# Set 0's block merge and the first units' decay factors on VectorE, with a new set of ranks

## The chip, the cores and the metric

One core of a Trainium2 chip. The metric is the device time of one execution, in microseconds; the kernel before takes 836.14 us (median of 3 runs, 835.84 to 836.43).

## The reference, cut to what matters

A recurrence over 768 time steps for 4 batches of 8 heads (head size 40), and behind it a two-part MLP with residuals.

```
for t in range(S):                                    # r k v w a b: (4, 8, 768, 40)
    y[:, :, t] = einsum('bhd,bhde->bhe', r_t, state)
    Sa = einsum('bhde,bhe->bhd', state, a_t)
    state = state * w_t[:, :, None, :] - einsum('bhd,bhe->bhde', Sa, b_t) + einsum('bhd,bhe->bhde', v_t, k_t)
x = y.transpose(0, 2, 1, 3).reshape(4, 768, 320)
h = relu(x^T @ w_tok1) @ w_tok2                       # over the 768 time steps, 256 wide
u = x + h^T
out = u + relu(u @ w_ch1) @ w_ch2                     # over the 320 features, 1536 wide
```

## The kernel before, in words

The 768 steps of each batch are cut into 12 chunks of 64, so there are 48 chunks, numbered g. Inside a chunk the recurrence becomes matrix products; between chunks a state is handed on, so the chunks of a batch form a chain.

**Preparation (`t_prep`, line 473).** The chunks are prepared in three units of 16, each in four quarters of 16 steps. A quarter loads a tile `pin`, scans the decays to running products (line 542), forms the reciprocal decay factors RC in one first step (line 567) and seven steps, each the one after it times a decay (line 569), multiplies K and B with RC and A with the running products (all of them through `either`, line 415), and stores the results to DRAM. `p_rc`, `p_k` and `p_a` say for each unit which engine does the factors, the products of K and B, and that of A: 0 is VectorE, 1 is POOL, 2 is whichever of POOL and VectorE is free. Units 0 and 1 feed chunks 0 to 31.

**Sets (`t_solve`, line 929).** Chunks go in six sets of 8. For a set, the diagonal 32-blocks of a triangular matrix of each chunk and head, in the buffer `Dg`, are transposed on VectorE (line 945) and inverted there: 15 row steps, each a product and a sum (lines 968 and 970), give the two 16-blocks of each 32-block. Then the 16-blocks are merged to 32-blocks. For sets from `pem` on, VectorE does it: six left pairs (983, 985), one copy (1004) and six right pairs (996, 999), and then the transposes to TBt (1024) and TBn (1029); `Dg` is free for the next set as soon as it is transposed. For sets below `pem` (before: set 0 alone) the left and right pairs are left out, and `t_merge` (line 883) does the merge after the transposes with small matmuls (line 898), which VectorE evicts (904) and adds (921, 922); `Dg` is free for the next set only after the first of these matmuls. The steps of a set have ranks that rise evenly from the set's own rank over `solve_span`:

```
steps += [left(e, 4 * e, t, t + 8) for e in range(2) for t in (0, 8)] + [left(e, 4 * e, 0, 16) for e in (2, 3)]
steps += rows + [right(e, 4 * e, 4 * e + 4) for e in range(2)]
...
    yield rank0 + K["solve_span"] * u / len(steps)
```

**Chunks.** `t_ab` (751) loads a pair of chunks, transposes and multiplies (pk, pa, px); `t_a` (830) evicts to Dg, N and AT; `t_b` (1111) copies the set's inverse to TBD (line 1129 and on), forms the pe, pt and ph products and evicts them. `t_chain` (1224) is the chain over the chunks, in two halves of the heads; its first matmuls are line 1259. `t_y` forms the output of a pair of chunks. `t_v` (1092) copies v on an engine out of `vg`. `t_conv` (line 1465) splits the MLP's weights from 64-bit words on POOL, ScalarE, VectorE and TensorE (lines 1497 to 1516), and `t_mlp` runs the MLP of one batch, with most of its matmuls in lines 1642 and 1756.

**The order.** `Planner` (line 74) runs all of this as generators before anything is on the chip. Each operation has an engine, a length and the rank of its task. Step by step the engine that can start soonest takes the ready operation with the lowest rank (TensorE adds a price for a change of matmul form, `aff`, `affx`), and what it takes is issued: the order on every engine's queue is that of the plan. Lengths are the planner's own estimates. A length marked `Port` also keeps other operations so marked waiting until it ends, on VectorE or POOL. Where TensorE would stand in the plan, `fill` issues small matmuls to a spare bank (line 402). All ranks, spans and engine choices are in the dict `K`.

Of the kernel before, what the change touches and what calls it, by code (L numbers as in the profile page):

```python
# [23 lines left out]
LAT = {"PE": 190.0, "ACT": 210.0, "DVE": 130.0, "POOL": 150.0, "SP": 1000.0, "SWD": 1100.0}  # L24


K = dict(mgs=0, mgl=0, lat=[200.0, 150.0, 145.0, 90.0], aff=[2.14563, 1.17505], affx=[1.41848, 1.75913],
         aff_g=12.71949, sets=[8, 8, 8, 8, 8, 8], atn=6, kbp=2, ld=3.64466, ldk=-0.09022, v=5.95243, vg='PDA',
         tbd_early=55.14308, tbd=[['DP', 'AD', 'DP', 'PA'], ['AP', 'P', 'PD', 'AP']], alt_c=1, slack=-24704.48396,
         evm=31.10979, p_rc=[2, 2, 2], p_a=[0, 0, 2], p_k=[0, 0, 1], solve=[5.47355, 2.30103, 3.06635, -7.67957,  # L30
         3.37784, -15.13123], solve_span=13.30881, atomic=0, a=10.15159, a_span=3.80664, b=1.43321, chain=0.31813,
         evac=17.1625, y=-0.05033, utr=-7.4913, pem=1, mrg=-1.4447, ea=7.7058, prp=17, psp=8, w=3, c=2, m=2, warm=0,
         fill=2, prep=[-17.22917, -0.28798, 24.97603], prep_step=[1.61428, -1.4801, -0.20849], p_wg=[1, 3], p_big=[2],
         mlp=[11.95325, 26.40847, 34.1668, 39.83709], mlp_span=[14.39104, 11.00328, 13.05494, 18.79706],
         conv_t=5.14066, conv_t_span=3.01188, conv_c=5.76098, conv_c_span=7.60449, conv_after=4, cv_free=2, cvp=[1,
         2], ub=0, y_ld=5.29409, e_k=-39.43453, e_a=-28.4508, e_s=2.43935, e_x=-25.441, e_l=-7.61654)


class Port(float):
# [31 lines left out]
class Planner:  # L71
# [105 lines left out]
    def away(self, form, rank):  # L177
# [3 lines left out]
        late = rank >= K["aff_g"]  # L181
        return K["affx"][late] if "A" not in (form, self.form) else K["aff"][late]

# [78 lines left out]
def tile_kernel(ctx, tc, r, k, v, w, a, b, wt1, wt2, wc1, wc2, wakb, rvt, vtok, wl, out, dbg=None):  # L262
    nc = tc.nc
    B, H, S, D = r.shape
# [8 lines left out]
    DP = 104  # L273
# [11 lines left out]
    prep = rec.enter_context(tc.tile_pool(name="prep", bufs=2))  # L285
# [96 lines left out]
    P = Planner()  # L382
# [90 lines left out]
    def t_prep(u):  # L473
# [7 lines left out]
        now = yield pr0  # L481
        for q in range(NQ):
# [12 lines left out]
            if u == 1 and q == NQ - 1:  # L495
                now = yield None
# [7 lines left out]
            def comp(q=q, d=d, ring=ring, tsl=tsl):  # L504
# [5 lines left out]
                now = yield None  # L510
# [27 lines left out]
                def scan():  # L538
                    if not alt:
# [2 lines left out]
                    nc.vector.tensor_tensor_scan(  # L542
                        out=o["CP"].rearrange("p e t -> p (e t)"), data0=pin[:, 0:W1N],
                        data1=D1.rearrange("p e t -> p (e t)"), initial=0.0, op0=ALU.mult, op1=ALU.add)
                now = yield [("DVE", Port(250), carry), ("DVE", 1560, scan)]
                P.set(scan_ev[q], now)
                CP, ce, fl = d["CP"], o["ce"], o["fl"]

# [28 lines left out]
                now = yield [("ACT", 760, sq), ("DVE", Port(190), rec), ("DVE", 650, lambda: nc.vector.reciprocal(out=d["rq"], in_=d["rq"]))]  # L577
# [20 lines left out]
                now = yield None  # L598
                P.spawn(rest(), pr0 + q * prs, now)

                now = yield [("ACT", 1225, lambda: nc.scalar.copy(out=W, in_=Pv))]
                P.set(cp_free[q], now)
                yield ld_ev
                now = yield [either(eng_a, lambda: A, lambda: A, lambda: W, ALU.mult, 640)]
# [10 lines left out]
                now = yield None  # L615
# [7 lines left out]
            now = yield None  # L623
# [16 lines left out]
        now = yield [("ACT", 160, pcc), ("ACT", 160, pcc2)]  # L640
        P.rel(tk, now)
        P.rel(R_cp, now)
        for s_ in stored:
            yield s_
        now = yield None
        P.set(prep_done[u], now)
        yield 12.0 * u
        now = yield [("DVE", 402, lambda: nc.vector.tensor_reduce(out=fl[:, 4:5], in_=ce, axis=AX.XY, op=ALU.min)),
               ("DVE", 402, lambda: nc.vector.tensor_reduce(out=fl[:, 5:6], in_=ce, axis=AX.XY, op=ALU.max)),
               ("DVE", 73, lambda: nc.vector.tensor_reduce(out=fl[:, 6:7], in_=fl[:, 0:NQ], axis=AX.X, op=ALU.max)),  # L650
               ("DVE", 70, lambda: check(u, 0, fl[:, 4:5], ALU.is_ge, CMAX ** -2, HL)),
               ("DVE", 70, lambda: check(u, 1, fl[:, 5:6], ALU.is_le, CMAX ** 2, HL)),
               ("DVE", 70, lambda: check(u, 2, fl[:, 6:7], ALU.is_le, WMAX ** 2, HL))]
# [811 lines left out]
    def t_conv(i, key, shape, sW, data, r0, r1):  # L1465
# [8 lines left out]
        now = yield None  # L1474
# [6 lines left out]
        else:  # L1481
            n = DM if kind == "c2" else 384
# [3 lines left out]
        def piece(j, hc, lc, n):  # L1486
            yield r0 + (r1 - r0) * j / len(ps_)
            yield R_hid
            buf = mp.tile([128, 2 * 384], F32, tag="hid", name=f"cx_{key[0]}_{key[1]}_{j}", bufs=HIDN)
            x = buf.bitcast(I32)[:, 0:2 * n]  # L1490
            xv = x.rearrange("p (n two) -> p n two", two=2)
            c, l = t_[:, hc:hc + n], t_[:, lc:lc + n]
            hi = xv[:, :, 1].bitcast(F32)
            a0 = c_ + 128 * n * j
            yield [("SP", (480.0, 3.6 * n), lambda: nc.sync.dma_start(out=x, in_=wl[a0:a0 + 128 * n].bitcast(I32).rearrange("(p n) -> p n", p=128)))]
            hI = xv[:, :, 1]
            yield [[(e, ns, lambda e=e: engines[e].tensor_scalar(out=c, in0=hi, scalar1=0.0, scalar2=None, op0=ALU.mult))  # L1497
                    for e, ns in (("POOL", 900.0), ("DVE", Port(68 + n)))][:K["cvp"][0]]]
            yield [("ACT", 95 + 0.97 * n, lambda: nc.scalar.activation(out=hi, in_=hi, func=AF.Copy, scale=2.0 ** -112))]
            yield [("DVE", Port(dve(n)), lambda: nc.vector.scalar_tensor_tensor(out=hI, in0=hI, scalar=3, in1=c.bitcast(I32),  # L1500
                                                                          op0=ALU.logical_shift_left, op1=ALU.bitwise_or))]
            pt, tk = yield from bank("m", [128, 384], f"cv_{key[0]}_{key[1]}_{j}")
            yield [[("ACT", 95 + 0.97 * n, lambda: nc.scalar.copy(out=c, in_=hi)),
                    ("POOL", 700, lambda: nc.gpsimd.tensor_copy(out=c, in_=hi))][:K["cvp"][1]],
                   ("DVE", 68 + n, lambda: nc.vector.tensor_scalar(out=pt[:, 0:n].bitcast(I32), in0=hI, scalar1=-0x800000, scalar2=None,
                                                                   op0=ALU.bitwise_and))]
            yield [("DVE", 60 + n / 0.96, lambda: nc.vector.scalar_tensor_tensor(
                out=l, in0=xv[:, :, 0].bitcast(U32), scalar=-2.0 ** -52, in1=pt[:, 0:n], op0=ALU.mult, op1=ALU.mult))]

            def mm(q):  # L1510
                a_, b_ = ((ident, hi), (nid, c), (nid, l))[q]
                return ("PE", (670, 1640, "A") if q == 0 else (173, 507, "A"),
                        lambda: nc.tensor.matmul(pt[:, 0:n], lhsT=a_, rhs=b_, start=q == 0, stop=q == 2))  # L1513
            now = yield [mm(q) for q in range(3)]
            P.rel(R_hid, now)
            now = yield [("ACT", act(n), lambda: nc.scalar.copy(out=l, in_=pt[:, 0:n]))]
            P.rel(tk, now)
            left[0] -= 1
            if left[0] == 0:
                P.set(cv_ev[key], now)  # L1520
                now = yield [("SP", (480.0, data), lambda: nc.sync.dma_start(out=sW.bitcast(F32), in_=t_.bitcast(F32)))]
                P.set(cv_st[key], now)
        now = yield None
# [478 lines left out]
```

## Time and profile before

| | |
|---|---|
| median of the runs | 836.14 us |
| the profiled execution | 840.57 us, span 838.9 us, mean granted clock 0.966 |
| TensorE busy, with filler | 792.3 us (94%) |
| VectorE busy | 563.7 us (67%) |
| ScalarE busy | 429.4 us (51%) |
| POOL busy | 167.7 us (20%) |
| filler matmuls (line 402) | 85.7 us |

Busy times are sums over the profiled execution. TensorE's share contains the filler, which computes nothing that is used, so the share alone does not say how much of the time is needed; the windows by stage and those of line 402 together do. In the rows PE is TensorE, DVE VectorE, ACT ScalarE, SP the queue that issues most DMAs. The granted clock is a share of full speed.

### The profile page before, as it was taken

What the parts mean: (1) busy time and instruction counts of PE and PEld (TensorE: products, weight loads), DVE (VectorE), ACT (ScalarE), POOL (GpSimd) and SP (SyncE); (2) the same over time, 40 slices, a digit from 0 to 9 for tenths busy, and PEclk for the clock granted to TensorE, in tenths of its full rate; (3) what the DMA queues carried; (4) which work ended last, traced back from release to release, by engine and by line L of the source; (5) the groups of instructions that cost most, each with busy time, mean ns of one, the idle gap of its engine ahead of it and who ended that gap; (6) DMA issues with size and microseconds to landing.
All of it is one profiled execution on the core that took longest, in us unless ns stands there. A gap on an engine that the chain in (4) does not pass through costs nothing.

```text
span 838.9 us, 31729 instructions
## 1 busy us (share of the span) xinstructions
PE 792.3 (94%) x13602; PEld 693.0 (83%) x13602; DVE 563.7 (67%) x1341; ACT 429.4 (51%) x1279; POOL 167.7 (20%) x276
## 2 busy tenths in 40 slices
PE   8896899999899899999999999999999999999997
PEld 7796777788788678687888888888888988989997
DVE  7665599986789689984566995449975444535332
ACT  3420497467668684545575665644464343433111
POOL 7300143002403461513220111011121010000000
PEclk9998699999899899999999999999999999999999
DMA  9586277887676846637457754552566345434331
GB/s 345 185 223 149 54 256 238 218 181 203 151 204 172 285 174 165 177 93 179 146 140 207 230 173 100 141 145 92 174 171 201 82 109 138 129 124 170 119 137 51
DMA packets 179027, 139.08 MB, mean 166 GB/s; under 512 B 146112, under 2 KB 154560, under 8 KB 175808
## 3 DMA queue, kind: packets, MB, share of 16 engines
q1 hardware_dynamic: 174128, 101.59, 44.4%
q0 software_dynamic: 4752, 35.39, 12.3%
q8 instruction: 109, 1.79, 0.9%
q14 instruction: 38, 0.31, 0.1%
HBM read 102.55 MB, written 34.41 MB: 163 GB/s over the span
## 4 chain that ended last, share of the span: by engine, by line
PE 65%; DVE 12%; ACT 4%; issue 3%; DMA 1%; SPq 1%; POOL 0%; ACTq 0%; DVEq 0%
PE m L1642 19%; PE m L1756 15%; PE cv_c L1513 3%; PE pq L1284 3%; PE yb L402 2%; PE pq L1259 2%; PE yb L1415 2%; PE ph L1193 2%; PE pU L290 2%; PE pq L1279 2%; PE px L816 2%; PE yb L1419 2%; PE pS L1344 2%; PE pk L290 1%; PE pt L1168 1%
## 5 line engine op out<-in xcount | busy, mean ns | idle before, releaser
L1764 ACT ACTIVATE hd<-m 128x384 fp32r<-128x384 f32 x96 | 47.2, 491 | 171.4 <-PE m L1756 171.2
L1756 PE MATMUL m<-ut,wg_c 128*128 128x384 f32 x576 | 122.5, 346 | 0.0
L1642 PE MATMUL m<-wg_c,hd 128*128 128x320 f32 x648 | 110.3, 314 | 1.3 <-DVE x L1794 0.7
L1642 PEld LDWEIGHTS m<-wg_c,hd 128*128 128x128 f32 x648 | 97.6, 188 | 4.9 <-DVE hd L1766 1.4
L1756 PEld LDWEIGHTS m<-ut,wg_c 128*128 128x128 f32 x576 | 97.4, 188 | 3.0 <-issue 0.4
L1794 DVE TENSOR_TENSOR x<-m,x 128x320 f32<-128x320 f32 x96 | 46.9, 489 | 67.7 <-PE m L1642 67.3
L402 PE MATMUL yb<-ident 128*128 128x192 bf16 x773 | 85.7, 257 | 2.5 <-POOL ident masks.py:199 1.7
L1766 DVE SCALAR_TENSOR_TENSOR hd<-m,hd 128x384 fp32r<-128x384 f32 x96 | 53.3, 555 | 45.6 <-ACT hd L1764 44.7
L402 PEld LDWEIGHTS <-ident 128*128 128x128 bf16 x773 | 67.0, 102 | 11.0 <-issue 3.9
L1134 POOL COPY TBD<-TBt 32x256 f32<-32x256 f32 x43 | 32.9, 765 | 121.4 <-PE ph L1193 92.9
L857 ACT ACTIVATE Dg<-px 128x128 f32<-128x128 f32 x132 | 35.7, 270 | 17.8 <-PE px L816 7.5
L1642 PE MATMUL m<-cv_c,hd 128*128 128x320 f32 x216 | 39.0, 323 | 2.2 <-DVE x L1794 2.1
L1756 PE MATMUL m<-ut,cv_c 128*128 128x384 f32 x192 | 40.9, 345 | 0.1
L1578 POOL DMA_DIRECT2D wg_c<-sW_c x24 | 13.1, 544 | 133.2 <-PE m L1642 77.3
L1415 PE MATMUL yb<-KB,RM 128*64 128x40 f32 x768 | 38.1, 223 | 0.5 <-DVE RM L1315 0.4
L1358 ACT ACTIVATE UB<-pS,PCt 40x40 f32<-40x40 f32 x144 | 30.7, 281 | 14.7 <-PE pS L1346 8.2
L1274 ACT COPY UB<-pq 104x256 f32<-104x256 f32 x96 | 31.4, 377 | 11.3 <-PE pq L1259 10.7
L1642 PEld LDWEIGHTS m<-cv_c,hd 128*128 128x128 f32 x216 | 32.9, 192 | 4.6 <-DVE x L1794 2.9
L787 ACT COPY KBT<-pk 104x512 f32<-104x512 f32 x40 | 23.4, 586 | 24.6 <-PE pk L290 24.4
L1497 POOL TENSOR_SCALAR cv_c<-cx_c 128x384 fp32r<-128x384 f32 (+1 forms) x24 | 28.7, 1203 | 33.5 <-DMA cx_c<-in_wl_dram 30.1
L1259 PEld LDWEIGHTS pq<-RV 40*64 40x64 f32 x768 | 28.6, 136 | 7.7 <-issue 4.8
L1259 PE MATMUL pq<-RV 40*64 40x64 f32 x768 | 34.8, 225 | 0.0
(220 smaller groups left out, 1857.8 us busy)
## 6 DMA issues: line engine op xcount, KB each, us to landing
wg_c<-sW_c POOLq DMA_DIRECT2D x12, 1152.0 KB, 6.7
pin<-in_wakb_dram SPq DMA_DIRECT2D x12, 960.0 KB
wg_c<-sW_c POOLq DMA_DIRECT2D x12, 960.0 KB, 4.9
RV<-in_rvt_dram SPq DMA_DIRECT2D x48, 208.0 KB
sKB<-pin SPq DMA_DIRECT2D x12, 640.0 KB
KB<-sKB SPq DMA_DIRECT2D x48, 160.0 KB
wg_t<-sW_t POOLq DMA_DIRECT2D x6, 1152.0 KB, 5.8
KBp<-sKB SPq DMA_DIRECT2D x40, 160.0 KB
```

The lines of the kernel that those rows point to most:

```text
L402: nc.tensor.matmul(yb[:, 320:512], lhsT=zf[:, 0:128], rhs=zf[:, 0:192], start=True, stop=True)
L857: act_ = ("ACT", 250, lambda: nc.scalar.activation(out=o_, in_=i_, func=AF.Copy, scale=-1.0))
L1134: "P": ("POOL", 740, lambda: nc.gpsimd.tensor_copy(out=dst, in_=src))}
L1259: nc.tensor.matmul(pqs[g][z][0][c0:c1, j, D:DP], lhsT=l_, rhs=rb[z * 64:z * 64 + D, j, :], start=True, stop=True)
L1274: yield [("ACT", 330, lambda: nc.scalar.copy(out=hv(G)[:, :, D:DP], in_=d["pq"][0:DP, :, D:DP]))]
L1358: return ("ACT", 175, lambda: nc.scalar.activation(out=hv(getG(g + 1))[64:DP, p, 0:D], in_=d["pS"][0:D, p], func=AF.Copy, scale=PCt[u][0:D ...
L1415: nc.tensor.matmul(py[g - 1][z * 64:z * 64 + 64, h, :], lhsT=rms[g - 1 + z][:, h, :], rhs=o["kb"][:, h, :], start=h == 2 * j, stop=False)
L1642: nc.tensor.matmul(d[key], lhsT=lhs(i, a_), rhs=rhs(i, b_), start=i == 0 and j == 0, stop=i == n - 1 and j == 2)
L1756: nc.tensor.matmul(pt, lhsT=mm_[q][0], rhs=mm_[q][1], start=q == 0, stop=q == len(mm_) - 1)
L1764: nc.scalar.activation(out=hid[key][:, 0], in_=pt, func=AF.Relu)
L1766: now = yield [("DVE", dve(384), lambda: nc.vector.scalar_tensor_tensor(out=hid[key][:, 1], in0=pt, scalar=0.0, in1=hid[key][:, 0].bitcast ...
L1794: now = yield [("DVE", dve(320), lambda: tt(out=x()[:, i], in0=d[("c2", g, i)], in1=x()[:, i], op=ALU.add))]
```

## The change

`pem` goes from 1 to 0, so set 0 is merged on VectorE as the others are, and `t_merge` is not used. `p_rc` goes to VectorE alone for units 0 and 1; `p_a` of unit 1 goes to POOL and that of unit 2 to VectorE; `p_k` of unit 2 goes from POOL to either. `vg` loses POOL. `tbd` gets two other lists of engines. The scan's length becomes 1570 ns, marked `Port`, and POOL's first step of a conversion 1120 ns, both in the planner alone. Nearly all ranks and spans have new numbers. What is computed stays the same.

```
--- before.py
+++ after.py
@@ -24,16 +24,16 @@
 LAT = {"PE": 190.0, "ACT": 210.0, "DVE": 130.0, "POOL": 150.0, "SP": 1000.0, "SWD": 1100.0}
 
 
-K = dict(mgs=0, mgl=0, lat=[200.0, 150.0, 145.0, 90.0], aff=[2.14563, 1.17505], affx=[1.41848, 1.75913],
-         aff_g=12.71949, sets=[8, 8, 8, 8, 8, 8], atn=6, kbp=2, ld=3.64466, ldk=-0.09022, v=5.95243, vg='PDA',
-         tbd_early=55.14308, tbd=[['DP', 'AD', 'DP', 'PA'], ['AP', 'P', 'PD', 'AP']], alt_c=1, slack=-24704.48396,
-         evm=31.10979, p_rc=[2, 2, 2], p_a=[0, 0, 2], p_k=[0, 0, 1], solve=[5.47355, 2.30103, 3.06635, -7.67957,
-         3.37784, -15.13123], solve_span=13.30881, atomic=0, a=10.15159, a_span=3.80664, b=1.43321, chain=0.31813,
-         evac=17.1625, y=-0.05033, utr=-7.4913, pem=1, mrg=-1.4447, ea=7.7058, prp=17, psp=8, w=3, c=2, m=2, warm=0,
-         fill=2, prep=[-17.22917, -0.28798, 24.97603], prep_step=[1.61428, -1.4801, -0.20849], p_wg=[1, 3], p_big=[2],
-         mlp=[11.95325, 26.40847, 34.1668, 39.83709], mlp_span=[14.39104, 11.00328, 13.05494, 18.79706],
-         conv_t=5.14066, conv_t_span=3.01188, conv_c=5.76098, conv_c_span=7.60449, conv_after=4, cv_free=2, cvp=[1,
-         2], ub=0, y_ld=5.29409, e_k=-39.43453, e_a=-28.4508, e_s=2.43935, e_x=-25.441, e_l=-7.61654)
+K = dict(mgs=0, mgl=0, lat=[200.0, 150.0, 145.0, 90.0], aff=[2.8149, 1.61617], affx=[1.53709, 1.00236], aff_g=7.75127,
+         sets=[8, 8, 8, 8, 8, 8], atn=6, kbp=2, ld=1.95737, ldk=-1.12926, v=7.61727, vg='AD', tbd_early=44.91461,
+         tbd=[['DP', 'DA', 'DP', 'PA'], ['AP', 'D', 'AP', 'DA']], alt_c=1, slack=-24712.17031, evm=48.06334, p_rc=[0,
+         0, 2], p_a=[0, 1, 0], p_k=[0, 0, 2], solve=[5.0068, 2.39429, 3.83284, -7.65883, -0.85338, -17.6322],
+         solve_span=14.59011, atomic=0, a=10.25014, a_span=3.82403, b=1.33979, chain=0.05899, evac=32.00926,
+         y=-0.53356, utr=7.99716, pem=0, mrg=-3.61051, ea=7.86942, prp=18, psp=8, w=3, c=2, m=2, warm=0, fill=2,
+         prep=[-19.56133, -0.25654, 25.19342], prep_step=[1.28967, -2.84269, 3.94421], p_wg=[1, 3], p_big=[2],
+         mlp=[11.95325, 26.73624, 34.09528, 44.371], mlp_span=[14.28833, 10.73503, 13.14326, 20.28331],
+         conv_t=8.13548, conv_t_span=4.07889, conv_c=8.26868, conv_c_span=13.68438, conv_after=1, cv_free=2, cvp=[1,
+         2], ub=0, y_ld=4.68843, e_k=-35.73709, e_a=-23.39785, e_s=1.76137, e_x=-32.8848, e_l=-7.37276)
 
 
 class Port(float):
@@ -542,7 +542,7 @@
                     nc.vector.tensor_tensor_scan(
                         out=o["CP"].rearrange("p e t -> p (e t)"), data0=pin[:, 0:W1N],
                         data1=D1.rearrange("p e t -> p (e t)"), initial=0.0, op0=ALU.mult, op1=ALU.add)
-                now = yield [("DVE", Port(250), carry), ("DVE", 1560, scan)]
+                now = yield [("DVE", Port(250), carry), ("DVE", Port(1570), scan)]
                 P.set(scan_ev[q], now)
                 CP, ce, fl = d["CP"], o["ce"], o["fl"]
 
@@ -1495,7 +1495,7 @@
             yield [("SP", (480.0, 3.6 * n), lambda: nc.sync.dma_start(out=x, in_=wl[a0:a0 + 128 * n].bitcast(I32).rearrange("(p n) -> p n", p=128)))]
             hI = xv[:, :, 1]
             yield [[(e, ns, lambda e=e: engines[e].tensor_scalar(out=c, in0=hi, scalar1=0.0, scalar2=None, op0=ALU.mult))
-                    for e, ns in (("POOL", 900.0), ("DVE", Port(68 + n)))][:K["cvp"][0]]]
+                    for e, ns in (("POOL", 1120.0), ("DVE", Port(68 + n)))][:K["cvp"][0]]]
             yield [("ACT", 95 + 0.97 * n, lambda: nc.scalar.activation(out=hi, in_=hi, func=AF.Copy, scale=2.0 ** -112))]
             yield [("DVE", Port(dve(n)), lambda: nc.vector.scalar_tensor_tensor(out=hI, in0=hI, scalar=3, in1=c.bitcast(I32),
                                                                           op0=ALU.logical_shift_left, op1=ALU.bitwise_or))]
```

## Rows read from the trace of the kernel before

**Rows 1.** Windows by stage: length, busy us (count) of each engine, granted clock, DMA share, GB/s

```profile
0.00:45.00 45.00, 37.82 (x704) 34.79 (x707) 31.15 (x64) 17.85 (x35) 22.19 (x56) 0.96 0.74 260
...
71.50:97.10 25.60, 16.67 (x816) 14.94 (x816) 10.77 (x21) 4.13 (x13) 1.84 (x6) 0.58 0.20 44
...
97.10:104.20 7.10, 6.67 (x187) 5.63 (x190) 4.50 (x8) 5.32 (x10) 1.86 (x2) 0.83 0.54 121
...
104.20:189.00 84.80, 80.30 (x1597) 65.65 (x1588) 78.53 (x175) 58.51 (x162) 20.46 (x28) 0.96 0.82 224
...
189.00:294.00 105.00, 95.57 (x1991) 80.37 (x1992) 78.69 (x185) 74.82 (x223) 30.69 (x41) 0.93 0.74 204
...
294.00:756.00 462.00, 451.55 (x7365) 392.19 (x7354) 307.19 (x757) 247.16 (x782) 85.55 (x130) 0.99 0.52 149
```

**Rows 2.** Windows by stage, the filler matmuls of line 402 alone

```profile
104.20:189.00 84.80, 13.36 (x116) 10.12 (x116) 0.96 0.82 224
...
189.00:294.00 105.00, 9.58 (x80) 6.83 (x80) 0.93 0.74 204
...
294.00:756.00 462.00, 13.89 (x116) 9.40 (x117) 0.99 0.52 149
```

**Rows 3.** Timeline of TensorE: start us, length us, engine, line, operation, count

```profile
88.12 1.13 PE L816 MATMUL px<-KBT,ATB 40*64 40x128 f32 x16
...
97.13 0.67 PE L1143 MATMUL pe<-TBt,N 32*32 32x32 f32 x32
...
103.33 1.10 PE L816 MATMUL px<-KBT,ATB 40*64 40x128 f32 x32
...
104.25 0.22 PE L1259 MATMUL pq<-RV 40*64 40x64 f32 x2
```

**Rows 4.** Timeline of VectorE from set 0's last row step into its merge

```profile
70.86 0.62 DVE L970 TENSOR_REDUCE Tl<-tmp 128x30 f32<-128x450 f32 x1
...
71.52 1.90 DVE L1024 STREAM_TRANSPOSE TBt<-Tl 128x1024 f32<-128x1024 f32 x1
...
73.34 1.21 DVE L1029 STREAM_TRANSPOSE TBn<-Tl 128x1024 f32<-128x1024 f32 x1
...
83.41 0.42 DVE L921 TENSOR_TENSOR TBt<-me,TBt 128x256 f32<-128x256 f32 x1 [3.31 <-PE me L898]
```

**Rows 5.** Windows over set 1's left and right steps: lines 983, 985, 1004, 996, 999

```profile
158.80:184.10 25.30, 3.96 (x6) 0.87 0.85 210
...
158.80:184.10 25.30, 3.58 (x6) 0.87 0.85 210
...
158.80:184.10 25.30, 0.37 (x1) 0.87 0.85 210
...
158.80:184.10 25.30, 3.60 (x6) 0.87 0.85 210
...
158.80:184.10 25.30, 3.57 (x6) 0.87 0.85 210
```

**Rows 6.** Window of line 569, first 45 us; VectorE's wait (total, times, longest)

```profile
0.00:45.00 45.00, 3.27 (x11) 12.42 (x17) 0.96 0.74 260
...
DVE pin L415 <- POOL RC L569: 3.7, 2, 2.6
```

**Rows 7.** Lines 569, 1500 in windows; line 415 by form; one scan

```profile
84.00:140.00 56.00, 6.58 (x20) 3.40 (x8) 0.86 0.55 173
...
104.20:189.00 84.80, 4.70 (x8) 0.96 0.82 224
...
L415 POOL TENSOR_TENSOR pin<-pin,RC 128x640 f32<-128x640 f32 x8 | 12.7, 1582 | 2.2 <-PE ph L1193 1.9
...
L415 DVE TENSOR_TENSOR pin<-pin 128x640 f32<-128x640 f32 x12 | 10.1, 844 | 2.0 <-ACT pin L601 2.0
...
102.27 2.32 DVE L542 TENSOR_TENSOR_SCAN CP<-pin,D 128x680 f32<-128x680 f32 x1
```

**Rows 8.** Waits of SP's queue, 58 to 105 us

```profile
SPq L418 <- PE pk L290: 24.9, 1, 24.9
```

## The prediction

> **What bounds the kernel now.** I read the stage windows first, then the filler alone in the same windows, then the timelines of VectorE and TensorE where they showed a hole, and last the waits. The profiled execution took 840.57 us (span 838.9), 4.4 us over the median of the runs (836.14); the sum below is made against 840.57 and then taken from the median.
>
> The windows [rows 1] show two kinds of time. From 294 us on TensorE is busy 451.6 of 462 us and VectorE 307: matrix work sets the pace, and only 13.9 us of it is filler, the matmuls the planner puts in gaps [rows 2]. Before 294 us TensorE has less to do than its row says: 13.4 us of filler and 4.5 idle in the 84.8 us from 104.2, and 9.6 and 9.4 in the 105 after them [rows 1, 2]. The rest of the early loss is a wait for the first set. The stretch from 71.5 to 97.1 is the emptiest of the run: TensorE 16.7 of 25.6 us, VectorE 10.8, ScalarE 4.1, DMA 0.20, the clock granted 0.58, so mostly the lower of its two levels [rows 1]. What runs there is the merge of set 0 on TensorE.
>
> So what is saved before the first chain step (104.25 [rows 3]) is saved at the end, if the work in between keeps its length: behind it comes a queue of matrix work that is nearly full.
>
> **The change part by part.**
>
> *Merge of set 0 on VectorE (pem 0).* Before: the last row step ends at 71.48, the transposes take 1.90 and 1.21 us, and then VectorE waits for small matmuls again and again, 3.31 us at one place [rows 4]. The first block product of the chain, the pe matmul of line 1143, starts at 97.13 [rows 3]: 25.6 us after the last row step. After: six left pairs, a copy and six right pairs stand between row steps and transposes. Another set shows them, line by line: 3.96 + 3.58 + 0.37 + 3.60 + 3.57 = 15.1 us [rows 5]. With the transposes that is 18.2, so 7.4 us sooner if VectorE does nothing else in between. It had 10.8 us of work in this stretch, 3.1 of it the transposes and some 2.5 the six evictions and adds of the merge, at 0.42 [rows 4]; the other 5.2, put in between, leave a gain of 2.2. I take **-5**. The copies to TBD follow as before.
>
> *Clock.* The px matmuls take 1.13 us for 16 at 88.12 and 1.10 for 32 at 103.33 [rows 3]: half speed while the merge's small matmuls and their gaps run. Without them filler stands there, as before 71.5. The path from the first pe to the first chain step, 7.1 us at a granted 0.83, would be 5.9 at full clock: **-1** (ends: 0, and -2 with the transposes before it).
>
> *Decay factors of units 0 and 1 on VectorE (p_rc).* The diff sets both to VectorE alone. In unit 0 POOL had 17 of the 28 steps of line 569, 12.42 us of them, against 3.27 for 11 on VectorE: 0.73 against 0.30 each [rows 6]. VectorE gets 5.1 us more and loses 3.7 of waiting for POOL before its products [rows 6]; the chain of one quarter gets shorter by 0.43 a step. VectorE is busy 31.2 of the first 45 us, so there is room. Ends: -3.7 (all the wait, work in idle time) and +1.4 (the work on the path). I take **-1.5**: the wait is a gain as a whole only if nothing else holds the same products, and evictions and copies of ScalarE do.
>
> *VectorE from 104 to 189.* It is busy 78.5 of 84.8 us, and this stage it bounds [rows 1]. Unit 1's eight POOL steps come to it, 8 x 0.33 = +2.6; unit 1's product of A goes to POOL, 4 x 0.84 = -3.4 [rows 7]. The conversions of the token weights get a later rank (8.1 for 5.1); eight pieces of line 1500 are 4.70 us here [rows 7], with two more such steps each some 14. They have to be done before the first MLP, so between 0 and -14 leaves this stage; I take -2. Also, without TensorE's merge the set's diagonal buffer is free after its transpose, and SP does not stand 24.9 us behind the pk transposes with set 1's loads queued behind them [rows 8]; not priced. Together **-3**, ends -15 and +7.
>
> The upper end has unit 1's four products on POOL, at 1.58 each, hold VectorE up instead of running beside it, which is a rival below.
>
> *Ranks, the scan as a port user, POOL's 1120 for 900, v copies without POOL, unit 2's products on either engine.* These change the order the planner writes, not the arithmetic. TensorE's idle and filler from 189 to 294, 19 us, is what a better order could take at most; a worse one can make more of 294 to 756 look like that: 45 us of it at 18% loss in place of 5% is +6. **0**, for no row says which.
>
> Sum: -5 - 1 - 1.5 - 3 = -10.5; 840.6 becomes 830.1, and the median 836.1 becomes **826**.
>
> **The rivals.**
>
> *VectorE is the bound, and unit 1 goes ahead of set 0 (slower).* The new steps are ranked after the row steps: set 0's 28 steps run from -5.0 to 9.1 in equal shares, so the left and right ones stand at 2.8 and above. Unit 1's quarters stand at -0.3, -3.1, -5.9 and -8.8, and whatever of them is ready goes first. A quarter is scan 1.57, eight steps of 0.30 to 0.33, two products of 0.84 [rows 7] and about a microsecond of small ones: some 6.7 us, 27 in all. Before, nothing could be pushed back this way, since the rest of the merge was TensorE's. If all four go first the chain starts 27 - 7 = 20 us later; VectorE then has that work behind it in the full stage, where I give back 13. Price +7: **843**. It decides from about 13 us of unit 1 before set 0's last right step. For it: a VectorE at 93% that gets work [rows 1]. Against it: a quarter waits for ScalarE between its scan and its copy, so the left and right steps slip in, and the loads come late. The Trainium skill, page "Perfetto Trace Analysis", section "Optimizing Scalar/DVE Operations", would say that where VectorE is saturated work may go to ScalarE or even GpSimd, which is the other way from this change. Chance 0.22.
>
> *The order gains too.* The conversions leave the full stage wholly (-14 in place of -2), and the order of 189 to 294 gives back a few more: **812**. For it: 19 us of filler and idle there. Against it: the first MLP needs those weights. Chance 0.14.
>
> *The products on POOL take it back (no change).* Unit 1's four products of A move to POOL beside a VectorE that is full. If VectorE stands while they run, they cost it 4 x 1.58 = +6.3 in place of -3.4 [rows 7], and the sum shrinks from -10.5 to -0.8: **835**. For it: a scan that is about 1.57 elsewhere took 2.32 us at 102.27, with POOL at work beside it [rows 7]. Against it: that is 0.75 of a delay, not a whole product. The Trainium skill, page "SBUF — State Buffer", section "Who interferes with whom", says that a VectorE instruction with two SBUF inputs and a GpSimd instruction that reads SBUF shut each other out for the whole length of whichever came first. By that rule the stretched scan is a scan that began late, and every product of unit 1 would cost in full when it comes first. Chance 0.08.
>
> **How the numbers follow.** Forecast 0.56 (its own range 819 to 834), gains in order 0.14, no change by POOL 0.08, slower 0.22. About 0.2% is what a measurement of this kernel tells from no change, 834.5 to 837.8. Faster 0.56 + 0.14 = 0.70; same 0.08; slower 0.22. The range, 813 to 842, leaves out half of the second case (0.07) and half of the slower one (0.11).
>
> **What would show it.** Right: the stretch after set 0's row steps has a granted clock near 1.0, no line 898, the first pe matmul some 18 to 23 us after the last row step, and the first chain step near 94 instead of 104; no wait of VectorE for POOL in the first 45 us; set 1's transposes before 182. Wrong in size: the chain starts sooner and the stages after it are longer by the same amount. Wrong in sign: scans of unit 1 between the left steps of set 0, the first chain step after 110, or products on POOL with scans beside them at 2 us and more. If the chain starts near 94, and the span from there to the end is longer than 734 us, it is the ranks and not the merge that decided.

## The result and the profile after

The kernel after takes 816.27 us (median of 4 runs, 813.27 to 818.27), the kernel before beside it 835.99: a ratio of 0.9765 [0.9731, 0.9798] (the brackets hold the 95% interval), 19.7 us less. The forecast was 826 with a range of 813 to 842, so the sign is right, and the saving is nearly twice the 10.5 us of the sum. It lies outside the 819 to 834 of the forecast's own case; the stated range holds it because it was widened for the rival that stood at 812. The profiled execution of after took 815.92 us, so it stands at its median; that of before stood 4.4 us above its own. The two profiles therefore differ by 24.7 us, and some 5 of these are the executions that happened to be profiled.

The page of after, the span and the first part (engine, busy us, share of the span, instructions), and the group of the filler (line 402):

```profile
span 814.1 us, 30499 instructions
...
PE 781.8 (96%) x12990; PEld 687.3 (84%) x12990; DVE 578.7 (71%) x1386; ACT 436.8 (54%) x1296; POOL 141.5 (17%) x226
...
L402 PE MATMUL yb<-ident 128*128 128x192 bf16 x929 | 99.4, 252 | 1.7 <-POOL ident masks.py:199 1.6
```

TensorE's needed time is its busy time without the filler: 792.3 - 85.7 = 706.6 us before, 781.8 - 99.4 = 682.4 after. What is left of the span, filler and idle together, is 132.3 and 131.7. On this count the difference lies in TensorE's needed time. The count is rough: the filler's busy time overlaps with other matmuls in the trace. The matmuls of all other lines, taken together, cover 725.7 us of the span before and 705.6 after, 20 of the 24.8 us by which the spans differ. And it says where time went, not why.

The windows of after at the stage cuts of [rows 1]; the columns are the same:

```profile
0.00:45.00 45.00, 40.29 (x800) 36.76 (x804) 33.41 (x82) 19.10 (x38) 9.88 (x42) 0.96 0.77 265
...
71.50:97.10 25.60, 22.56 (x372) 20.53 (x369) 23.73 (x46) 13.60 (x35) 4.58 (x5) 0.93 0.46 118
...
104.20:189.00 84.80, 80.18 (x1707) 65.93 (x1706) 78.01 (x179) 53.25 (x146) 18.41 (x17) 1.00 0.76 208
189.00:294.00 105.00, 100.42 (x2004) 83.08 (x2003) 87.32 (x201) 79.89 (x241) 33.60 (x46) 0.97 0.71 200
294.00:756.00 462.00, 452.92 (x7207) 399.62 (x7206) 307.40 (x767) 247.61 (x777) 67.16 (x105) 1.00 0.55 156
```

The emptiest stretch of before is full: from 71.5 to 97.1 VectorE is busy 23.7 us instead of 10.8, and the clock granted is 0.93 instead of 0.58, mostly the higher of its two levels. The stretch from 104.2 to 189 looks as before, VectorE 78.0 of 84.8, but more of the kernel's work has been done by its end.

VectorE's timeline of after (start, length, line, operation, tiles, count), from the last row step of set 0 to its transposes, to be held against [rows 4]:

```profile
67.89 0.61 DVE L970 TENSOR_REDUCE Tl<-tmp 128x30 f32<-128x450 f32 x1
...
68.75 0.68 DVE L983 TENSOR_TENSOR tmp_x<-DT,Tl 128x512 f32<-128x512 f32 x1
...
76.25 0.38 DVE L1004 COPY DT<-Tl 128x256 f32<-128x256 f32 x1
...
81.46 1.57 DVE L542 TENSOR_TENSOR_SCAN CP<-pin,D 128x680 f32<-128x680 f32 x1
...
86.33 0.68 DVE L999 TENSOR_REDUCE Tl<-tmp_y 128x32 f32<-128x512 f32 x1
...
87.13 1.95 DVE L1024 STREAM_TRANSPOSE TBt<-Tl 128x1024 f32<-128x1024 f32 x1
...
90.62 1.23 DVE L1029 STREAM_TRANSPOSE TBn<-Tl 128x1024 f32<-128x1024 f32 x1
```

The left pairs, the copy and the right pairs stand where the change puts them, from 68.75 to 87.0, with one scan of unit 1 and its first small steps between them. There is no gap of more than a microsecond. A scan of unit 1 among these steps was one of the prediction's signs of a wrong sign; the kernel is faster all the same.

TensorE's timeline of after, as in [rows 3], with the first pe matmul and the first chain step:

```profile
91.85 0.64 PE L1143 MATMUL pe<-TBt,N 32*32 32x32 f32 x32
...
99.90 0.27 PE L1259 MATMUL pq<-RV 40*64 40x64 f32 x1
```

The chain starts at 99.90, 4.35 us sooner than at 104.25. That is a sixth of the 24.8 us by which the spans differ. To see where the rest comes from, I cut both traces at the same events: the first chain step, chunk 8's eviction in the chain (line 1274, counted in order of time), chunk 16's, the last one, and the end. Chunk 8 is the first that needs set 1, chunk 16 the first that needs unit 1 and set 2. Before:

```profile
0.00:104.25 104.25, 87.20 (x2167) 80.81 (x2171) 66.64 (x157) 32.85 (x74) 27.33 (x70) 0.87 0.63 190
104.25:199.00 94.75, 90.07 (x1875) 74.25 (x1868) 85.52 (x193) 65.58 (x184) 23.28 (x33) 0.96 0.81 222
199.00:290.80 91.80, 82.56 (x1669) 68.87 (x1668) 69.54 (x160) 65.21 (x194) 27.08 (x35) 0.93 0.73 198
290.80:739.50 448.70, 438.84 (x7229) 379.98 (x7228) 303.21 (x748) 244.15 (x772) 84.75 (x129) 0.99 0.53 151
```

After, the same events:

```profile
0.00:99.90 99.90, 92.16 (x1676) 85.45 (x1676) 82.29 (x197) 43.49 (x104) 17.05 (x52) 0.97 0.71 214
99.90:185.60 85.70, 80.42 (x1727) 66.44 (x1721) 81.18 (x185) 55.52 (x153) 21.61 (x21) 1.00 0.76 214
185.60:270.50 84.90, 80.72 (x1712) 67.32 (x1715) 67.75 (x157) 63.52 (x195) 20.31 (x29) 0.96 0.70 183
270.50:716.60 446.10, 436.45 (x7235) 380.59 (x7228) 309.04 (x766) 253.07 (x792) 77.69 (x116) 1.00 0.57 160
```

So 4.35 us are saved up to the chain's start, 9.05 from there to chunk 8, 6.9 to chunk 16, 2.6 to the last chunk and 1.9 behind it. The 4.5 us behind chunk 16 are no more than what before's profiled execution stood above its median. The third column of busy times is VectorE's. It did 152.2 us of work up to chunk 8 before and 163.5 after, 11.3 more, and stood idle 46.8 us (37.6 and 9.2) before and 22.1 (17.6 and 4.5) after. So on VectorE the 13.4 us by which chunk 8 is sooner are 24.7 us of idle time less and 11.3 us of work more. That is a count; the experiments ask which edits did it.

### The profile page after: what moved, and what is told of

The parts are those of the page before. It is cut to its first block, busy times and chain, and to the rows that moved or that the text cites. A ratio compares the mean times of both kernels' runs of the same rounds, so it can differ in the third digit from the quotient of the medians.

```text
span 814.1 us, 30499 instructions
## 1 busy us (share of the span) xinstructions
PE 781.8 (96%) x12990; PEld 687.3 (84%) x12990; DVE 578.7 (71%) x1386; ACT 436.8 (54%) x1296; POOL 141.5 (17%) x226
## 3 DMA queue, kind: packets, MB, share of 16 engines
q0 software_dynamic: 4752, 35.39, 12.8%
## 4 chain that ended last, share of the span: by engine, by line
PE 64%; DVE 13%; ACT 4%; issue 3%; DMA 2%; POOL 0%; SPq 0%; DVEq 0%; ACTq 0%; POOLq 0%
PE m L1642 19%; PE m L1756 16%; PE pq L1284 3%; PE cv_c L1513 3%; PE ph L1193 2%; PE pq L1259 2%; PE yb L402 2%; DVE tmp L968 2%; PE pq L1279 2%; PE px L816 2%; PE yb L1415 2%; DVE Tl L970 2%; PE pS L1344 1%; PE pU L290 1%; PE pk L290 1%
## 5 line engine op out<-in xcount | busy, mean ns | idle before, releaser
L402 PE MATMUL yb<-ident 128*128 128x192 bf16 x929 | 99.4, 252 | 1.7 <-POOL ident masks.py:199 1.6
L402 PEld LDWEIGHTS <-ident 128*128 128x128 bf16 x929 | 77.7, 100 | 12.1 <-issue 4.6
L1134 POOL COPY TBD<-TBt 32x256 f32<-32x256 f32 x38 | 28.7, 755 | 139.6 <-DVE TBt L1024 90.7
L857 ACT ACTIVATE Dg<-px 32x128 f32<-32x128 f32 (+1 forms) x134 | 36.3, 271 | 23.1 <-PE px L816 14.1
L1578 POOL DMA_DIRECT2D wg_c<-sW_c x24 | 13.1, 547 | 173.5 <-PE m L1756 86.2
L1419 PE MATMUL yb<-STs,RV 104*64 104x80 f32 x384 | 33.9, 248 | 1.2 <-issue 1.2
L968 DVE TENSOR_TENSOR tmp<-Tl,DT 128x2 f32<-128x2 f32 (+14 forms) x90 | 33.5, 372 | 2.1
L1377 ACT COPY STs<-pU 40x160 f32<-40x160 f32 x88 | 25.0, 284 | 18.5 <-PE pU L290 16.9
L1756 PEld LDWEIGHTS m<-ut,cv_c 128*128 128x128 f32 x192 | 32.7, 188 | 1.7 <-ACT cv_c L1516 0.5
```

The lines of the kernel that those rows point to most:

```text
L402: nc.tensor.matmul(yb[:, 320:512], lhsT=zf[:, 0:128], rhs=zf[:, 0:192], start=True, stop=True)
L857: act_ = ("ACT", 250, lambda: nc.scalar.activation(out=o_, in_=i_, func=AF.Copy, scale=-1.0))
L968: lambda tmp: tt(out=vw(tmp), in0=tv[:, :, 0:t, 0:t], in1=dv[:, :, t, 0:t].unsqueeze(2).to_broadcast([128, 2, t, t]), op=ALU.mult),
L1419: nc.tensor.matmul(py[g - 1][z * 64:z * 64 + 64, 2 * j:2 * j + 2, :].rearrange("p h e -> p (h e)"), lhsT=o["rb"][:, j, :], rhs=o["sp"][:, ...
L1756: nc.tensor.matmul(pt, lhsT=mm_[q][0], rhs=mm_[q][1], start=q == 0, stop=q == len(mm_) - 1)
```

## The experiments

Times are medians of several executions, ratios are to the kernel before on the same chip. Lines of numbers in the diffs are entries of `K`, put in behind its definition, so that the lines of these kernels are one higher in their rows. Times at chunks are from one profiled execution each. The two kernels that were profiled twice agree with themselves within 2.2 us at chunk 8 and 0.9 us at chunk 16 and behind it.

**One part of the change undone.** Set 0's merge on TensorE again, in the kernel after:

```
+ K.update(pem=1)
```

> The kernel after, with set 0 merged on TensorE again (pem 1), all else as after. Theory A (the gain comes from VectorE being kept at work while set 0 is solved, and set 1's blocks being evicted meanwhile, since the diagonal buffer is free at once): the granted clock of the merge stretch falls below 0.75 again, set 1's transpose moves back from 108 towards 130 us, and at least half of the gain of 19.7 us is lost: 826 to 832 us. Theory B (the new ranks do it): only the direct piece is lost, the first pe matmul 2 to 5 us later, 818 to 822 us.

Measured: 829.07 us, 0.9918 [0.9882, 0.9954], 12.8 above after. The window between its last row step and its first pe matmul:

```profile
68.29:97.51 29.22, 17.83 (x826) 16.15 (x826) 11.30 (x24) 4.15 (x13) 1.79 (x2) 0.59 0.44 133
```

VectorE's timeline in it, with what ended the idle time in brackets:

```profile
76.63 0.48 DVE L905 TENSOR_SCALAR DT<-me,half 128x256 f32<-128x256 f32 x1 [4.45 <-PE me L899]
...
82.89 0.42 DVE L922 TENSOR_TENSOR TBt<-me,TBt 128x256 f32<-128x256 f32 x1 [5.77 <-PE me L899]
```

The hole is back: VectorE busy 11.3 of 29.2 us, waits of 4.45 and 5.77 us for the small matmuls, the clock at 0.59. The same stretch is 23.35 us in after, so in this pair the merge is worth 5.9 us on the way to the chain. Chunk 8 is at 202.2 instead of 185.6, so another 11 us are lost by then, with 46.3 us of idle VectorE ahead of it, as before. Chunk 16 is 17.8 us later than in after, and behind it some 4.6 us are won back. The time lies in the range of theory A.

The decay factors and products of before:

```
+ K.update(p_rc=[2, 2, 2], p_a=[0, 0, 2])
```

> The kernel after, with the decay factors of units 0 and 1 on POOL or VectorE again and the products of A of units 1 and 2 as before (p_rc, p_a of before), all else as after. Theory A: the first row steps of set 0 start about 3 us later as before, and VectorE has 5 to 8 us less work up to the first chain step, which gives part of it back: 817 to 821 us. Theory B: as A, 816 to 819. A third, that POOL's steps beside VectorE were the loss throughout the early stage: 825 or more.

Measured: 824.46 us, 0.987 [0.9831, 0.991], 8.2 above after. Here the plan lets scans of unit 1 go ahead of set 0's transposes (at 79.0, 90.6 and 101.6; the second transpose ends at 106.9), and the chain starts at 114.3, 14.4 us later than in after. Chunk 16 is only 5.7 later, at 276.2. The time lies in none of the three ranges expected. The end of set 0's row steps doesn't move back: 68.0, with POOL doing 14 of the 28 steps of line 569 in the first 45 us.

**Structure and ranks apart.** The engine choices of after in the kernel before, with its ranks:

```
+ K.update(pem=0, p_rc=[0, 0, 2], p_a=[0, 1, 0], p_k=[0, 0, 2], vg='AD',
+          tbd=[['DP', 'DA', 'DP', 'PA'], ['AP', 'D', 'AP', 'DA']], tbd_early=44.91461, prp=18)
```

> The kernel before, with all the engine choices of after (pem, p_rc, p_a, p_k, vg, tbd, tbd_early, prp) but the ranks, spans and planner lengths of before. Theory A: more than half of the gain: 818 to 826 us, set 1's transpose before 120. Theory B: little of it: 830 to 838 us.

And the ranks and lengths of after with the engine choices of before:

```
+ K.update(pem=1, p_rc=[2, 2, 2], p_a=[0, 0, 2], p_k=[0, 0, 1], vg='PDA',
+          tbd=[['DP', 'AD', 'DP', 'PA'], ['AP', 'P', 'PD', 'AP']], tbd_early=55.14308, prp=17)
```

> The kernel after, with all the engine choices of before (pem 1, p_rc, p_a, p_k, vg, tbd, tbd_early, prp) but the ranks, spans and planner lengths of after. Theory A: little of the gain: 829 to 838 us, set 1's transpose later than 125. Theory B: most of it: 818 to 824 us.

Measured: the structure alone 830.6 us, 0.9909 [0.9878, 0.994]; the ranks alone 823.72, 0.9859 [0.9818, 0.99]. Against the 837.61 of before beside them that is -7.0 and -13.9; by the ratios 0.9 and 1.4%, which together make the 2.3% of the whole change. Both times lie in the ranges of theory B, that the ranks do it. The windows of the ranks alone, from the first chain step at 104.3 to chunk 8 and on to chunk 16:

```profile
104.30:190.30 86.00, 82.81 (x1762) 67.60 (x1765) 81.66 (x183) 60.72 (x170) 24.56 (x37) 0.98 0.81 222
190.30:273.80 83.50, 78.34 (x1676) 65.64 (x1668) 71.82 (x160) 61.83 (x187) 27.32 (x39) 0.96 0.66 185
```

With the merge still on TensorE, and the chain starting when it does in before, these two stages are as short as in after: 86.0 and 83.5 us, against 85.7 and 84.9 there and 94.75 and 91.8 before. So the ranks alone bring chunk 16 forward by 17.0 of the 20.3 us that the whole change does, and behind it they change nothing (548.2 us, before 548.1). The merge by itself can't claim its 12.8 us either: undoing all engine choices at once costs 7.5 us, less than undoing the merge alone. The choices and the ranks depend on one another, and the shares of the gain hold only for the combination in which they were measured.

VectorE's timeline of the structure alone:

```profile
77.13 1.57 DVE L543 TENSOR_TENSOR_SCAN CP<-pin,D 128x680 f32<-128x680 f32 x1
...
86.49 1.99 DVE L1025 STREAM_TRANSPOSE TBt<-Tl 128x1024 f32<-128x1024 f32 x1
...
103.23 2.78 DVE L543 TENSOR_TENSOR_SCAN CP<-pin,D 128x680 f32<-128x680 f32 x1
...
117.65 1.84 DVE L543 TENSOR_TENSOR_SCAN CP<-pin,D 128x680 f32<-128x680 f32 x1
...
119.86 1.23 DVE L1030 STREAM_TRANSPOSE TBn<-Tl 128x1024 f32<-128x1024 f32 x1
```

Its windows at the events (first chain step, chunks 8 and 16, end):

```profile
0.00:127.70 127.70, 120.30 (x1973) 110.66 (x1974) 110.09 (x260) 56.59 (x136) 29.03 (x62) 0.99 0.72 229
127.70:207.00 79.30, 75.23 (x1754) 64.58 (x1748) 62.38 (x142) 47.79 (x134) 16.68 (x24) 0.91 0.72 178
207.00:290.30 83.30, 78.69 (x1590) 64.92 (x1592) 71.90 (x160) 63.24 (x195) 20.77 (x32) 0.98 0.66 187
```

This is nearly the slower rival of the prediction. Only the first of unit 1's four quarters goes ahead of set 0's last right step; but all four go ahead of its second transpose, and the chain starts at 127.7, 23.5 us later than before (the prediction worked out 20). And the kernel is 0.9% faster than before. Chunk 16 comes at 290.3, where before has 290.8, and what the kernel wins lies behind it (540.8 us for 548.1). Up to the chain's start VectorE did 110.1 us of work instead of 66.6, and behind it there was so much less left that the 23.5 us were made up by chunk 16. Why the stage behind chunk 16 is shorter isn't shown.

The pages of these kernels also split the gain (TensorE busy without line 402, and the rest of the span):

| kernel | needed TensorE us | filler and idle us |
|---|---|---|
| before | 706.6 | 132.3 |
| structure alone | 685.8 | 145.3 |
| ranks alone | 698.2 | 123.8 |
| after | 682.4 | 131.7 |

By this rough count the structure takes 21 us out of TensorE's time, 11.9 of it line 898 itself, and gives 13 back as waiting; what the other 9 are isn't shown. The ranks take waiting away, 8.5 us, and as much of TensorE's time.

One group of ranks by itself, that of the conversions of the MLP's weights, in the kernel before:

```
+ K.update(conv_t=8.13548, conv_t_span=4.07889, conv_c=8.26868, conv_c_span=13.68438, conv_after=1)
```

> The kernel before with only the ranks of the weight conversions of after (conv_t 8.1 for 5.1, conv_c, their spans, conv_after 1). Theory C with the token weights' conversions (13.5 us on VectorE between chunks 0 and 8) as the work that moves back: chunk 0 to chunk 8 shorter than 90 us (94.7 in before), and 3 to 8 us faster than before. If it is the other ranks: within 2 us of before.

Measured: 823.07 us, 0.9836 [0.9806, 0.9866], 13.3 below before: these five numbers alone do as much as all the ranks together. The gain is neither where it was looked for nor where all the ranks have it. Its windows at the events:

```profile
104.85:197.05 92.20, 87.89 (x1846) 72.14 (x1838) 84.81 (x193) 63.72 (x179) 25.70 (x37) 0.96 0.81 219
197.05:287.30 90.25, 85.60 (x1726) 72.25 (x1721) 71.90 (x163) 65.27 (x197) 31.30 (x42) 0.96 0.71 202
287.30:822.30 535.00, 518.90 (x7832) 459.25 (x7823) 337.53 (x825) 265.54 (x831) 87.08 (x134) 1.00 0.52 151
```

Up to chunk 16 it saves 3.5 us (287.3 against 290.8), and behind it 13.1: 535.0 against 548.1 (838.9 less 290.8). The conversions don't leave the full stage: from 104.2 to 189 this kernel has 8 pieces of line 1500, and after has 7, where before has the 8 of [rows 7].

**Is it VectorE's work ahead of chunk 8?** The left and right steps of one set are issued twice, which changes no result; once for set 1, which chunk 8 waits for (`i == 1`), and in a second kernel for set 4 (`i == 4`):

```
-  return [("DVE", Port(60 + n_ * fac), f), ("DVE", 62 + n_ * 1.04, lambda: red(hold["t"]))]
+  ops = [("DVE", Port(60 + n_ * fac), f), ("DVE", 62 + n_ * 1.04, lambda: red(hold["t"]))]
+  return ops * (2 if i == 1 and ("_x" in nm or "_y" in nm) else 1)
```

> The kernel after, with each left and right step of set 1 done twice (15 us more on VectorE between the chunks 0 and 8, nothing on another engine). Theory C (up to chunk 16 the time is VectorE's work plus its idle time, and in the kernel after only 4.5 of the 86 us between chunk 0 and chunk 8 are idle): chunk 8 comes 9 to 15 us later, and the whole takes 8 to 15 us more than after. Theory D (what counts is when the chain starts; from there TensorE sets the pace): 0 to 4 us more.

> The kernel after, with each left and right step of set 4 done twice (the same 15 us on VectorE, between 434 and 490 us, where TensorE is full and VectorE idle for a third of the time). Theories C and D: 0 to 3 us more than after. If it costs as much as the doubling in set 1, the stage of the work is not what matters, and C falls.

Measured: set 1 twice 828.68 us, 0.9911 [0.9878, 0.9945], 12.4 above after; set 4 twice 823.31, 0.9829 [0.9784, 0.9874], 7.0 above after by the medians and 5.4 by the ratios, whose intervals overlap. Set 1 twice at the events:

```profile
0.00:96.90 96.90, 90.87 (x1679) 84.47 (x1680) 80.69 (x197) 43.55 (x104) 18.25 (x52) 0.98 0.73 221
96.90:200.40 103.50, 98.75 (x1967) 83.51 (x1968) 100.33 (x224) 66.10 (x179) 26.88 (x27) 1.00 0.77 208
```

Chunk 8 is at 200.4 instead of 185.6: 14.8 us later, with the chain started 3 us sooner than in after. VectorE did 17.5 us more up to there (181.0 for 163.5), some 14 of them the second steps, and was idle 2.7 us less. Chunk 16 is 15.9 later. With set 4 twice, chunks 8 and 16 are where they were (185.4, 270.8), and what it costs comes later. So ahead of chunk 8 the work of VectorE counts in full, whenever the chain starts. If set 4's 5 us are real, when 0 to 3 was expected, then cover behind chunk 16 is thinner than VectorE's share there (307 of 462 us) makes one think.

A larger number for set 1 in `solve`, which gives its steps a sooner rank:

```
+ K.update(solve=[5.0068, 6.0, 3.83284, -7.65883, -0.85338, -17.6322])
```

> The kernel after, with set 1's solution ranked 3.6 chunks earlier (solve[1] 6.0 in place of 2.39). In the kernel after chunk 8 waits some 9 us for set 1. If that wait is a loss of its own, chunk 8 comes 4 to 9 us sooner and the whole is 3 to 8 us faster than after. Theory C: the wait is only where VectorE's queue shows, VectorE's work and idle time up to chunk 16 stay the same, and the whole is within 3 us of after.

Measured: 817.04 us, 0.9757 [0.9712, 0.9801], as after. Set 1's second transpose ends at 178.0 (178.2 in after), chunk 8 is no sooner (188.3). Here a sooner place in the order moved nothing.

**Is it set 1's early start?** In after, set 1's diagonal blocks are transposed at 108.05, before at 137.69, because `Dg` is free after set 0's first transpose. Here it is free only after set 0's last two, nearly as late as in before:

```
-            if i >= PEM:
+            if i > 0:
                 P.set(Dg_free[i + 1], now)
...
                 now = yield [("DVE", 1810, o1), ("DVE", 1158, o2)]
+            if i == 0:
+                P.set(Dg_free[1], now)
```

> The kernel after, with the diagonal buffer given to set 1 only when set 0 is solved, instead of right after set 0's transpose; no work added or taken. Theory C with set 1's blocks as the work that fills VectorE's early idle time: VectorE's idle time before chunk 8 grows by 5 us or more, set 1's transpose moves from 108 to 115 or later, and the whole takes 4 to 10 us more than after. If the early evictions of set 1 are not what counts: within 3 us of after.

Measured: 811.5 us, 0.9698 [0.9649, 0.9747]. The early start is worth nothing here: without it, with set 1's transpose at 130.0, the kernel is faster. The explanation by it fell here. Once more, with the kernel after beside it on one chip:

> The kernel of e_dg_late once more (the diagonal buffer goes to set 1 only when set 0 is solved), beside the kernel after on the same chip. If it is faster than after by itself: 3 to 8 us faster in this pair too, with the gain behind chunk 16 as in its first profile. If the first result was chance: within 2 us of after.

> The kernel after once more, beside e_dg_late2 on the same chip: ratio to the kernel before 0.973 to 0.980, as at first.

Measured: 811.02 us, 0.9698 [0.9673, 0.9722], against 815.79, 0.9769 [0.9741, 0.9797]. The intervals don't meet: this version beats both kernels, after by 4.8 us. Of the first run's profile, chunk 8 is at 186.6 and chunk 16 at 272.6, both a little later than after's 185.6 and 270.5; the gain is behind chunk 16 (536.6 us against 543.6).

**The planner's lengths.** The scan no port user again, and POOL's step 900 ns:

```
- now = yield [("DVE", Port(250), carry), ("DVE", Port(1570), scan)]
+ now = yield [("DVE", Port(250), carry), ("DVE", 1560, scan)]
...
-   for e, ns in (("POOL", 1120.0), ("DVE", Port(68 + n)))][:K["cvp"][0]]]
+   for e, ns in (("POOL", 900.0), ("DVE", Port(68 + n)))][:K["cvp"][0]]]
```

> The kernel after with the planner's two lengths of before (the scan not a port user, POOL's conversion step 900 ns). Theory C: no work moves between engines, so only the order differs: within 4 us of after. If the truer lengths are what the new order rests on (scans beside POOL's work held up in a plan that does not know it): 5 to 12 us slower than after, and more scans longer than 1.8 us.

Measured: 820.0 us, 0.9803 [0.9773, 0.9834], 4.2 above the second measurement of after on the same chip; the intervals overlap. But the scans aren't longer for it: their mean is 1.63 us, and 1.75 in after. Chunk 16 is even sooner (264.1), and the loss is behind it, 553.9 us against 543.6. In this pair the mark doesn't keep the scans short; it moves the order, as a rank does.

## Why the prediction was right, and where its sizes were off

**The row steps (forecast -1.5).** They end at 68.50 instead of 71.48, so -3.0, near the lower end of -3.7. Line 569 in the first 45 us has no step on POOL any more, as against [rows 6]:

```profile
0.00:45.00 45.00, 8.00 (x28) 0.00 (x0) 0.96 0.77 265
```

28 steps take 8.00 us on VectorE, 0.29 each, and the wait for POOL is gone. But the -3.0 can't be credited to that move: with the factors of before and the ranks of after, where POOL still does 14 of the 28 steps, the row steps end at 68.0 and 68.1 (decay factors undone; ranks alone). With the new engine choices and the ranks of before they end at 67.3. So either edit moves it, and the two don't add up. The size is in the range; that POOL's wait was its cause isn't shown for the whole change.

**The merge (forecast -5).** From the last row step to the first pe matmul it is 23.35 us after and 25.65 before, -2.3, the weak end of -2.2 to -7.4: VectorE's other work, a scan and the px evictions, stands between the left and right steps as that bound assumed. Against the same kernel with the merge on TensorE it is -5.9. The -5 lies between the two, and the steps are those of [rows 5]. Of the signs, line 898 is gone, set 1's transposes end at 178.2 (said: before 182), and the pe matmul comes just behind the 18 to 23 us.

**The clock (forecast -1).** The clock is 1.00 there, as said, and the path from pe to chain step is longer all the same, 8.05 us for 7.12. The chain step needs ScalarE's evictions of the ph products (line 1204). These, and the matmuls around the chain's start, after:

```profile
97.40 1.06 ACT L1204 COPY UB<-ph 104x512 f32<-104x512 f32 x2
...
98.30 1.10 PE L816 MATMUL px<-KBT,ATB 40*64 40x128 f32 x32
99.33 0.64 PE L1143 MATMUL pe<-TBt,N 32*32 32x32 f32 x32
```

Before:

```profile
102.63 1.08 ACT L1204 COPY UB<-ph 104x512 f32<-104x512 f32 x2
...
104.81 0.41 PE L1143 MATMUL pe<-TBt,N 32*32 32x32 f32 x16
```

From the first pe matmul to the end of these evictions it is 6.61 us after and 6.58 before, at a granted 1.00 and 0.83: this part didn't scale with the clock, as the estimate had it. Behind it the chain step comes 1.44 us later instead of 0.54. TensorE first runs px and the next pair's pe matmuls, 0.64 us, and before those pe matmuls came behind the chain step. The +0.9 is this order.

So the chain's start moved by -3.0 - 2.3 + 0.9 = -4.4, where the sum had -7.5 and "near 94". The time to the chain's start has the sign of the forecast and a little over half of its size.

**The products on POOL (part of the -3; a rival at 0.08).** POOL's timeline of after has the four:

```profile
95.48 1.54 POOL L415 TENSOR_TENSOR pin<-pin 128x640 f32<-128x640 f32 x1 [3.30 <-ACT pin L601]
...
109.60 1.54 POOL L415 TENSOR_TENSOR pin<-pin 128x640 f32<-128x640 f32 x1 [6.49 <-ACT pin L601]
...
126.15 1.54 POOL L415 TENSOR_TENSOR pin<-pin 128x640 f32<-128x640 f32 x1
...
136.17 1.89 POOL L415 TENSOR_TENSOR pin<-pin 128x640 f32<-128x640 f32 x1 [8.48 <-ACT pin L601]
```

Each holds one VectorE instruction until it ends. VectorE's timeline:

```profile
95.68 1.41 DVE L536 COPY D<-CP 128x40 f32<-128x40 f32 x1
...
109.96 1.24 DVE L536 COPY D<-CP 128x40 f32<-128x40 f32 x1
...
125.98 0.18 DVE L536 COPY D<-CP 128x40 f32<-128x40 f32 x1
126.19 2.92 DVE L542 TENSOR_TENSOR_SCAN CP<-pin,D 128x680 f32<-128x680 f32 x1
...
137.06 1.16 DVE L968 TENSOR_TENSOR tmp<-Tl,DT 128x128 f32<-128x128 f32 x1
```

The copies that start at 95.68 and 109.96 end at 97.09 and 111.20, and the products at 97.02 and 111.14; such a copy is 0.18 when POOL is free. The scan at 126.19 ends at 129.11, which is the product's end, 127.69, and a scan's 1.57 behind it, within 0.15. The row step at 137.06 takes 1.16 for the 0.29 of the same shape in set 0. Together 1.23 + 1.06 + 1.35 + 0.87 = 4.5 us, so what was priced at -3.4 is +1.1. The Trainium skill's page "SBUF — State Buffer", section "Who interferes with whom", states it as an exclusive lock with whoever is second blocked for the whole instruction, and the trace agrees. The rival's mechanism is real, at 4.5 of its 6.3 us; it was too small to take the rest back. The scan of 2.92 us beside a product was also one of the signs of a wrong sign, and didn't mean one here.

**VectorE from 104 to 189 (forecast -3) and the ranks (forecast 0).** These are the steps that failed. To chunk 16 the two stages behind the chain's start give 16 us, and with the ranks alone they give 17.0. In the whole time the ranks by themselves are worth 11.8 by their ratio (1.41% of 836). "0, for no row says which" was the mis-sized term; its bound, -19, held. Five ranks of the conversions alone give 13.3, and none of it by leaving the full stage, which is how I had priced them. So the right sign came in part from the terms that were priced, 4.4 us at the chain's start, and for the larger part from one priced at nothing: that the time fell inside the stated range was luck more than working. By its time the rival at 812 is nearer than the forecast. Of its two reasons the conversions leaving the full stage isn't what happened; a better order, the other one, is what the ranks alone show, from the chain's start on and not only from 189.

**The premise.** "What is saved before the first chain step is saved at the end" doesn't hold. Structure alone starts the chain 23.5 us later and is faster; set 1 twice starts it 3 us sooner than after and is 12 slower. The first chain step is one point in a queue that VectorE works off, and up to chunk 8 the runs agree with a count of VectorE's work and idle time: with the ranks alone it is 152.4 us of work, as before, and 37.9 idle instead of 46.8, and chunk 8 is 8.7 us sooner. The slower rival's mechanism, seen in the structure alone, was nearly right, and its price was wrong: what goes ahead of the transposes is work that chunk 16 and those behind it need anyway, and much of it was done in VectorE's idle time. The prediction gave back 13 of 20 us; all of it had come back by chunk 16. The last test of the prediction, a span from the chain's start above 734 us if ranks decide, looked for a loss there; it is 714.2, a gain (before 734.6), and the ranks alone have 717.7.

**What stays open.** Behind chunk 16 the same work takes 535 to 554 us in these kernels, with the same arithmetic and a TensorE clock of 0.99 to 1.00. That is as large as the whole effect of the change, and the runs show which edits move it (the conversions' ranks, when `Dg` is free, the planner's lengths, the engine choices), not by which wait. Nor is it shown by which waits the ranks shorten the two stages ahead of chunk 16. Every edit also changes the planner's order behind it, so none of these runs moves one thing alone. Why before's profiled execution stood 4.4 us above its median wasn't followed up.

## What to carry to other kernels

When one engine is nearly full behind a point and half idle ahead of it, count its work and its idle time up to a later point that everything needs, instead of the time at which the next chain begins: a start that comes 23 us later cost nothing here, while some 14 us of extra work in the full stretch cost 12. Work that waits on another engine in small steps (a merge by 768 matmuls with VectorE evicting between them) can be worth moving onto the busier engine, since it removes waits and needed time at once. Where a planner orders everything, change its ranks alone and the structure alone as two kernels before giving the credit to either: here the ranks had 1.4 of the 2.3%, with intervals that overlap the structure's, and the two parts were not independent.

## What the runs showed of the hardware

That POOL's product of two SBUF tiles stops a VectorE copy with a single input of 128x40 for as long as it lasts (0.18 us becomes 1.24 and 1.41), not only scans and two-input operations, I had not expected. And the small matmuls of the merge cost little beyond their own time on TensorE. With the merge back and all else as in after, TensorE's needed time is 14.5 us longer by the count above (785.4 - 88.5 = 696.9, against 682.4), and line 898 (899 there) is 11.8 of it, so 2.7 us are left for all other matmuls. The 8.9 us that the structure alone takes off beyond line 898 therefore don't come from the merge alone. The clock granted in the first 100 us is 0.86 in before and 0.97 in after; from set 0's last row step to the first pe matmul it is 0.59 with the merge back and 0.93 in after.
